# Attention read by state, then a squared-ReLU MLP, on one core: heads grouped by parity, w_in kept decoded on chip, scores and W2 of all batches in float32 on 64x32 tiles

## The chip, the cores and the metric

The kernel runs on one core of a Trainium2 chip. The core has a matrix engine (TensorE, PE in the profile, with its weight loads as PEld), a vector engine (VectorE, DVE), a scalar engine (ScalarE, ACT), a third elementwise engine (GpSimd, POOL) and SyncE (SP), which issues DMAs. Each engine takes its instructions strictly in the order in which they stand in its own queue; engines wait for one another with semaphores. Working memory is SBUF (128 partitions); matmul results go to PSUM, which this kernel uses as eight banks of 128 x 512 float32. The metric is the device time of the launch in microseconds.

## The reference

There are 8 batches of 8 heads, 512 tokens and 32 states per head, head width 64. `x` and `state` are float32, the two MLP weights are float64 (the launch passes them as pairs of 32-bit words).

```python
scores = scale * np.matmul(x, state.transpose(0, 1, 3, 2))      # [B,H,512,32]
a = softmax(scores);  xread = np.matmul(a, state)               # [B,H,512,64]
scores2 = scale * np.matmul(state, x.transpose(0, 1, 3, 2))     # [B,H,32,512]
a2 = softmax(scores2); sread = np.matmul(a2, x)                 # [B,H,32,64]
attn = np.concatenate([xread, sread], axis=2)                   # 544 rows per batch
x = attn.transpose(0, 2, 1, 3).reshape(B * 544, 512)
h = np.maximum(x @ w_in, 0.0)                                   # w_in [512,2048]
return (h * h @ w_out).astype(np.float32)                       # w_out [2048,512]
```

## The kernel before

**Algebra.** For the token rows, `xread @ w_in` is the sum over heads of `a_h @ (state_h @ w_in_h)`. The kernel therefore makes, for each batch, a small weight W2 = `state_h @ w_in_h` for all heads (256 rows: 8 heads x 32 states; 2048 columns) and multiplies the softmax `a` (256 rows by 512 tokens, tiles `k_hi`, `k_lo`) with it. The 256 rows of `sread` of all batches form a ninth block, number 8, which is multiplied with `w_in` itself.

**Number format.** A value is kept as two fast-format (float32r) parts: hi, a cast by ScalarE, and lo, the rest, subtracted by VectorE or GpSimd (`split`, L301). `mm3` (L317) makes a product of three matmuls: hi·hi, hi·lo, lo·hi. A plain float32 matmul is issued as two instructions.

**The MLP.** Block `b` has 16 steps `hidden.b.fc` (L733) of 128 hidden units each: 6 matmuls of 512 columns into a PSUM tile `ph`, ReLU (L744 or L748), squaring (ScalarE L745, or VectorE L749), the cast `g_hi` (L750, ScalarE) and the subtraction `g_lo` (L751, VectorE). `accumulate.b.fc` then does 12 matmuls of 512 columns into four PSUM tiles `acc`, which stay open over the 16 steps. In blocks 0 and 1 only steps 0 to 7 run at first; their partial sums go to DRAM (`keep_part`) and steps 8 to 15 follow later.

**Weights.** `decode` (L328) turns the float64 words into float32: one ScalarE instruction and four VectorE instructions (L333 to L336) on 128x512. There are 16 pieces of `w_in` (`decode_wi.p`) and 16 of `w_out` (`decode_wo`, `prep_wo.fc`). The decoded `w_in` is written to DRAM (`win_d`) and read back later.

**W2.** It is made in four ways. Batches 0 and 1, first half: `direct_w2` (L593), plain float32 with a block-diagonal state of 64 columns, so that the two head pairs use the two 64-column halves of the array. Batches 0 and 1, second half, and batches 6 and 7: `paired_w2` (L615) with `mm3`, two batches at once, stored in DRAM (`w2a_d`). Batches 2 to 5: `quad_w2` (L690), four batches at once, stored in DRAM (`w2_d`). `load_w2` reads a batch's weight back for its block; for batches 2 to 5 it is split again.

**Attention of a batch**, in two halves `g` of four heads: `prep` transposes x, `scores` multiplies it with a block-diagonal state (float32 for batches 0 and 1; `mm3` of six matmuls per half for the others), `transposed_scores` (L425), `softmax` (L450 to L468) and `exp_s` make both softmaxes, `transposes` and `sread` the second read.

**Order of the work.** `PLAN` is a table, written by hand, of all these steps; the framework's scheduler starts from it and interleaves the instructions of neighbouring steps. `SECOND` says for many steps which of two engines is to do a part. Buffers come from rotating pools; a step waits for the readers of its buffer's last content.

Of the kernel before, what the change touches and what calls it, by code (L numbers as in the profile page):

```python
# [18 lines left out]

# [3 lines left out]


PLAN = """
    zero_bd.0.1 zero_bd.0.0 zero_bd.1.0 load_wo.1 ident load_raw.0 load_direct start.0 load_raw.1 states
        prep.0.0 scores.0.0 transposed_scores.0.0 softmax.0.0 decode_wi.0 load.0.1 zero_bd.1.1
        prep.0.1 scores.0.1 exp_s.0.0 direct_w2.0 start.1 decode_wi.1 load_wo.2 load_wo.0
        load_raw.2 decode_wi.2 direct_w2.1 load_wo.4 transposes.0.0 sread.0.0 load_raw.3 prep_wo.0
        direct_w2.2 decode_wi.3 transposed_scores.0.1 softmax.0.1 load_wo.3 load.1.1 exp_s.0.1  # L30
        transposes.0.1
    hidden.0.0 prep_wo.1 sread.0.1 prep.1.0 direct_w2.3 prep_wo.2
    hidden.0.1 scores.1.0 load_wo.5 transposed_scores.1.0 load_raw.4 decode_wi.4 prep.1.1 accumulate.0.0
        load_raw.5 load_wo.6 prep_wo.3 decode_wi.5
    hidden.0.2 direct_w2.4 scores.1.1 transposed_scores.1.1 load_wo.7 accumulate.0.1 softmax.1.0
        load_raw.6 decode_wi.6 
    hidden.0.3 load_raw.7 prep_wo.4 decode_wi.7 direct_w2.5 prep_wo.6
    hidden.0.4 direct_w2.6 prep_wo.5 load_wo.8 direct_w2.7 accumulate.0.2 exp_s.1.0
    hidden.0.5 load_wo.9
    hidden.0.6 accumulate.0.3 softmax.1.1 prep_wo.7 load_raw.8 accumulate.0.4 decode_wi.8 prep_wo.8  # L40
        load_quad.0 prep_quad.0
    hidden.0.7 zero_bd.0.2 load_wo.11 qprep.0.8 load_raw.9 decode_wi.9 qprep.0.9 load_wo.10 accumulate.0.5
    hidden.1.0 exp_s.1.1 prep_wo.9
    hidden.1.1 load_wo.12 accumulate.0.6 transposes.1.0 qw2.0.8 accumulate.1.0 load_raw.10 decode_wi.10
        accumulate.0.7 load_raw.11 decode_wi.11
    hidden.1.2 sread.1.0 start.2 prep_wo.10 qprep.0.10 load_raw.12 decode_wi.12 accumulate.1.1 qprep.0.11
        qw2.0.9
# [180 lines left out]

# [738 lines left out]
```

## Time and profile before

| | |
|---|---|
| median of 2 runs | 727.3 us (726.02 to 728.57) |
| profiled execution, its own time | 726.54 us |
| its span in the profile | 724.8 us |
| busy: PE, DVE, ACT, POOL | 95%, 60%, 56%, 29% of the span |
| mean granted clock of PE | 0.988 |
| DMA | 105.26 MB in 90644 packets, mean 145 GB/s |
| HBM read, written | 68.42 MB, 36.18 MB |

The profile is of one execution. A page gives the busy time of each engine, then the span in 40 slices of 18.1 us, in which a digit is the busy share in tenths. Shares over the whole span hide that the kernel has stages: the first 170 us, in which the weights are decoded, look different from the rest, so the stages are read from a table of windows. A row of a group reads: line, engine, operation, output<-inputs, shape, count | busy us in total, mean ns of one | idle time ahead of it and what ended it. The time of one matmul in such a row is its whole passage through the array; in a dense row of matmuls the next one starts earlier than the last one ends.

### The profile page before, as it was taken

How to read it: one execution, taken by the hardware profiler on the slowest of the kernel's cores; microseconds unless marked ns; L12 is line 12 of the kernel's file. 1: busy time of each engine (PE TensorE's matmuls, PEld its weight loads, DVE VectorE, ACT ScalarE, POOL GpSimd, SP SyncE). 2: the span in 40 equal slices, each digit the busy share in tenths (PEclk: the TensorE clock that was granted, in tenths of full speed). 3: DMA queues.
4: the chain of work that ended last, by engine and by line, in shares of the span. 5: the costliest groups of instructions: out<-in, count | busy, mean ns of one | idle time of the engine just before them, and what ended most of it. 6: DMA issues, size and time to landing. Idle time of an engine off the chain costs nothing.

```text
span 724.8 us, 9841 instructions
## 1 busy us (share of the span) xinstructions
PE 685.3 (95%) x3288; PEld 561.8 (78%) x3288; DVE 432.3 (60%) x749; ACT 403.2 (56%) x787; POOL 213.5 (29%) x183
## 2 busy tenths in 40 slices
PE   5787888989999999999999999999999999999997
PEld 2454676768888788888888888888888888888886
DVE  3999999998735685355634574457448333332233
ACT  4766756676655467655556575555455463344333
POOL 1133724355161336404531251226003131011100
PEclk9999799999999999999999999999999999999999
DMA  9744379896873655352335233543355233424102
GB/s 277 207 169 137 116 246 298 272 244 191 232 249 102 215 163 162 104 189 73 99 106 167 81 117 100 173 124 113 102 165 183 59 87 91 114 60 102 30 0 88
DMA packets 90644, 105.26 MB, mean 145 GB/s; under 512 B 24801, under 2 KB 61665, under 8 KB 90593
## 3 DMA queue, kind: packets, MB, share of 16 engines
q1 hardware_dynamic: 90592, 104.63, 47.7%
q8 instruction: 26, 0.43, 0.2%
q14 instruction: 26, 0.20, 0.1%
HBM read 68.42 MB, written 36.18 MB: 144 GB/s over the span
## 4 chain that ended last, share of the span: by engine, by line
PE 73%; DVE 13%; DMA 6%; issue 3%; SPq 2%; ACT 2%; POOL 0%; DVEq 0%; ACTq 0%
PE acc L322 42%; PE ph L322 22%; PE pr L322 2%; PE st L322 2%; DMA xp<-in_x_dram 2%; DVE deco L335 2%; PE w2ps L322 2%; DMA decq<-win_d 1%; DVE dec L335 1%; DVE deco L336 1%; DVE dec L336 1%; DVE deco L333 1%; DVE dec L333 1%; DMA wi_raw<-in_moe_w_in_dram 1%; DMA w_d<-qo 1%
## 5 line engine op out<-in xcount | busy, mean ns | idle before, releaser
L322 PE MATMUL acc<-wo,g_hi 128*128 128x512 f32 x1088 | 320.6, 395 | 7.8 <-ACT g_hi L750 5.6
L322 PEld LDWEIGHTS acc<-wo,g_hi 128*128 128x128 f32 x1088 | 202.8, 190 | 51.8 <-ACT g_hi L750 7.6
L322 PE MATMUL acc<-wo,g_lo 128*128 128x512 f32 x544 | 191.0, 391 | 0.0
L322 PE MATMUL ph<-k_hi,w 128*128 128x512 f32 x512 | 181.6, 395 | 4.8 <-DVE g_lo L751 4.6
L751 DVE TENSOR_TENSOR g_lo<-ph,g_hi 128x512 fp32r<-128x512 f32 (+1 forms) x144 | 94.4, 656 | 87.9 <-ACT g_hi L750 85.5
L749 DVE SCALAR_TENSOR_TENSOR ph<-ph,r 128x512 f32<-128x512 f32 (+1 forms) x98 | 65.3, 667 | 93.3 <-ACT r L748 93.0
L322 PEld LDWEIGHTS ph<-k_hi,w 128*128 128x128 f32 x512 | 96.4, 189 | 29.9 <-DVE g_lo L751 7.9
L322 PEld LDWEIGHTS acc<-wo,g_lo 128*128 128x128 f32 x544 | 101.0, 188 | 19.8
L750 ACT CAST g_hi<-ph 128x512 fp32r<-128x512 f32 (+1 forms) x144 | 81.2, 564 | 49.8 <-DVE ph L749 48.6
L748 ACT ACTIVATE r<-ph 128x512 f32<-128x512 f32 (+1 forms) x98 | 56.5, 577 | 84.0 <-PE ph L322 83.7
L322 PE MATMUL ph<-k_lo,w 128*128 128x512 f32 x256 | 100.5, 393 | 0.6 <-DVE k_lo L304 0.6
L322 PEld LDWEIGHTS ph<-k_lo,w 128*128 128x128 f32 x256 | 48.3, 189 | 9.9 <-DVE k_lo L304 1.1
L744 ACT ACTIVATE ph<-ph 128x512 f32<-128x512 f32 (+1 forms) x46 | 25.5, 555 | 37.3 <-PE ph L322 37.2
L304 POOL TENSOR_TENSOR wi<-decq,wi 128x512 fp32r<-128x512 f32 x16 | 21.7, 1356 | 76.7 <-ACT wi L303 76.7
L304 POOL TENSOR_TENSOR w<-w_f,w 128x512 fp32r<-128x512 f32 x20 | 25.9, 1293 | 51.7 <-ACT w L303 51.6
L304 POOL TENSOR_TENSOR s<-decs,s 128x512 fp32r<-128x512 f32 x12 | 15.4, 1293 | 80.9 <-ACT s L303 80.8
L687 POOL TENSOR_TENSOR tt<-decq,tt 64x512 fp32r<-64x512 f32 x16 | 23.5, 1472 | 41.2 <-ACT tt L684 17.2
L304 POOL TENSOR_TENSOR xn_lo<-xn,xn_hi 128x1024 fp32r<-128x1024 f32 x10 | 24.0, 2401 | 25.5 <-ACT xn_hi L303 24.6
L304 POOL TENSOR_TENSOR x_lo<-xT,x_hi 128x512 fp32r<-128x512 f32 x11 | 14.3, 1301 | 48.1 <-ACT x_hi L303 38.2
L517 ACT ACTIVATE srd<-pr,r 32x64 f32<-32x64 f32 x64 | 19.6, 306 | 14.4 <-PE pr L322 11.9
L304 POOL TENSOR_TENSOR wo<-deco,wo 128x512 fp32r<-128x512 f32 x13 | 18.4, 1416 | 28.1 <-ACT wo L303 15.2
L303 ACT CAST w<-w_f 128x512 fp32r<-128x512 f32 x32 | 19.7, 615 | 12.4 <-DMA w_f<-w_d 7.8
(123 smaller groups left out, 982.0 us busy)
## 6 DMA issues: line engine op xcount, KB each, us to landing
w<-w2a_d SPq DMA_DIRECT2D x48, 256.0 KB, 4.1
wo_raw<-in_moe_w_out_dram SPq DMA_DIRECT2D x16, 512.0 KB, 5.1
wi_raw<-in_moe_w_in_dram SPq DMA_DIRECT2D x16, 512.0 KB, 4.3
decq<-win_d SPq DMA_DIRECT2D x32, 256.0 KB, 3.0
w_d<-qo SPq DMA_DIRECT2D x64, 128.0 KB, 2.6
out_dram<-o SPq DMA_DIRECT2D x32, 256.0 KB, 3.8
w_f<-w_d SPq DMA_DIRECT2D x32, 256.0 KB, 2.8
w2a_d<-w2h SPq DMA_DIRECT2D x24, 256.0 KB, 3.0
```

The lines of the kernel that those rows point to most:

```text
L303: nc.scalar.copy(hi, src)
L304: pick(key, nc.gpsimd, nc.vector).tensor_sub(lo, src, hi.bitcast(F32))
L322: m = nc.tensor.matmul(ps, l, r, start=first and i == 0, stop=last and i == len(seq) - 1)
L333: nc.vector.tensor_scalar(vf, vf, F64_HI_MIN, F64_HI_MAX, ALU.max, ALU.min)
L335: nc.vector.scalar_tensor_tensor(v, high, 0xC0000000, v, ALU.bitwise_and, ALU.bitwise_or)
L517: nc.scalar.mul(srd[q].rearrange("p e d -> p (e d)"), pr[q, h], r2[q])
L687: eng.tensor_sub(t[v, :, i], wf[u], t[u, :, i].bitcast(F32))
L744: nc.scalar.activation(ph, ph, AF.Relu)
L748: nc.scalar.activation(r, ph, AF.Relu)
L749: nc.vector.scalar_tensor_tensor(ph, ph, 0.0, r, ALU.max, ALU.mult)
L750: nc.scalar.copy(ghi, ph)
L751: nc.vector.tensor_sub(glo, ph, ghi.bitcast(F32))
```

## The change

**What it does.** Heads are grouped by parity instead of by number: half `g` holds heads `g, g+2, g+4, g+6`. With that, the transposed state of all batches, `stT`, has in partitions 0 to 63 the even heads and in 64 to 127 the odd ones, and a head's state (64 rows, 32 columns) is one 64x32 tile of the array: two row halves by four column quarters. `scores` and the new `make_w2` issue eight float32 matmuls, one a head, in `by_head`, which pins them one behind the other, odd and even heads alternating and going to different PSUM banks. All of `w_in` stays decoded in SBUF (`wi`, four tiles), so `win_d`, `w2_d`, `w2a_d` and their DMAs go, as do the block-diagonal states, `direct_w2`, `paired_w2`, `quad_w2` and `load_w2`. A call of `make_w2` makes W2 of one batch for four steps (512 columns; 256 for the first four calls of batch 0). x is loaded for batches 2 to 7 twice, as before, now in 16 DMAs of 64 KB (`load_p`, pieces of 128 bytes) and one of 1 MB. The x of batch 0 is loaded through ScalarE's queue. The results of `sread` are moved between partitions by 16 DMAs within the chip (`move_sread`). PSUM keeps four banks for `acc`, two for `ph`, and gives the last two to one tile `psb`, of which there is a single buffer now, used in turn by scores, W2, transposes and `sread`. Block 8 now runs ahead of block 7, not interleaved with it. `accumulate.b.fc` stands one hidden step behind, where it stood two behind in the middle blocks.

```diff
-    hidden.0.0 prep_wo.1 sread.0.1 prep.1.0 direct_w2.3 prep_wo.2
+    hidden.0.0 load_raw.4 load_raw.5 load_wo.2 load_wo.3 start.1 load_n.1.0 load_n.1.1 load_n.1.2 load_n.1.3
...
+STATES = ((0, 2), (2, 3), (5, 3))
+OB, KB, XB, E2B, RB, WB, GB = 4, 2, 2, 2, 2, 2, 3
...
-    ps_b = ctx.enter_context(tc.tile_pool(name="ps_b", bufs=2, space=bass.MemoryType.PSUM))
+    ps_b = ctx.enter_context(tc.tile_pool(name="ps_b", bufs=1, space=bass.MemoryType.PSUM))
...
-    win_d = tc.dram_tile([NHB, NC // 2, P, 2, HB], F32, name="win_d")
-    w2_d = [tc.dram_tile([4, 4, Ns, G, HB], F32, name=f"w2_d{hb}") for hb in range(NHB)]
+    stT = cp.tile([P, B, NC, Ns], F32, tag="stT", name="stT")
+    wi = [cp.tile([P, NC, 2 * HB], F32, tag=f"wi{n}", name=f"wi{n}") for n in range(NHB // 2)]
...
+    def banks(name):
+        return ps_b.tile([P, 2, S], F32, tag="psb", name=name)
...
+    def by_head(jobs):
+        for i, (ps, l, r) in enumerate(jobs):
+            with tc.high_priority() if i else nullcontext():
+                m = nc.tensor.matmul(ps, l, r, start=True, stop=True)
+            if i:
+                tc.keep_in_program_order(m)
...
+        def load_p(self, j):
+            b = self.b
+            if j == 0:
+                self.xp = p2.tile([P, NC, J, 32], F32, tag="x", name=f"xp{b}", bufs=XB)
+            for h in range(2):
+                for e in range(E):
+                    o = 64 * h + 32 * e
+                    nc.sync.dma_start(
+                        self.xp[o : o + 32, j],
+                        x[b, 2 * j + h].rearrange("(t s) d -> s t d", s=32)[:, :, 32 * e : 32 * e + 32],
+                    )
...
+        def scores(self):
+            b = self.b
+            t = banks(f"sc{b}")
+            for g in range(G):
+                self.st[g] = t[:, g]
+            jobs = []
+            for j in range(NC):
+                for g in (1, 0):
+                    d, q = slice(64 * g, 64 * g + 64), slice(32 * j, 32 * j + 32)
+                    jobs.append((self.st[g][q], stT[d, b, j], self.xT[d, j]))
+            by_head(jobs)
...
+    def make_w2(b, hb, n):
+        if hb % 2 == 0:
+            w2t[b] = p2.tile([P, 2, G, 2, HB], F32R, tag="w2", name=f"w2_{b}_{hb}", bufs=WB)
+        u = slice(hb % 2, hb % 2 + n)
+        w = w2t[b]
+        t = banks(f"w2ps{b}_{hb}")
+        ps = [t[:, g, : n * HB].rearrange("p (u f) -> p u f", u=n) for g in range(G)]
+        jobs = []
+        for j in range(NC):
+            for g in (1, 0):
+                d, q = slice(64 * g, 64 * g + 64), slice(32 * j, 32 * j + 32)
+                r = wi[hb // 2][d, j, HB * (hb % 2) : HB * (hb % 2 + n)]
+                jobs.append((ps[g][q].rearrange("p u f -> p (u f)"), stT[d, b, j], r))
+        by_head(jobs)
+        for g in range(G):
+            split_v(w[:, u, g, 0], w[:, u, g, 1], ps[g])
...
+    def move_sread():
+        t = p2.tile([P, NC, B * Ns], F32, tag="wraw", name="srn", bufs=RB)
+        for g in range(G):
+            for e in range(E):
+                for j in range(NC):
+                    o = 64 * g + 32 * e
+                    nc.sync.dma_start(t[o : o + 32, j], srall[32 * j : 32 * j + 32, 2 * g + e])
+        hi, lo = [p2.tile([P, NC, B * Ns], F32R, tag=t, name=f"sr_{t}", bufs=KB) for t in ("k_hi", "k_lo")]
+        split_v(hi, lo, t)
...
+            pick(f"load_n.{b}.{k}", nc.sync, nc.scalar).dma_start(
+                self.xn[:, k], x[b, :, ts(k, P)].rearrange("h p d -> p h d")
+            )
```

**How it moves instructions.** Three places show it.

VectorE, around the subtraction `g_lo_6` of step 6 of block 0. In the kernel before this stands there (`dec` is a piece of `w_in` in decoding, `deco` one of `w_out`, `g_lo` the end of a hidden step):

```order
L335 SCALAR_TENSOR_TENSOR dec_745<-wi_raw_731,dec_745 128x512
L335 SCALAR_TENSOR_TENSOR deco_752<-wo_raw_636,deco_752 128x512
L336 SCALAR_TENSOR_TENSOR dec_745<-wi_raw_731,dec_745 128x512
L751 TENSOR_TENSOR g_lo_6_692<-ph_6_684,g_hi_6_691 128x512
L336 SCALAR_TENSOR_TENSOR deco_752<-wo_raw_636,deco_752 128x512
```

In the changed kernel the place looks so (`w_0_2` is a part of batch 0's W2, `sc_609` the scores of batch 1, `sp_0` and `xT` their transposes and those of x of batch 2):

```order
L293 SCALAR_TENSOR_TENSOR deco_1205<-wo_raw_1082,deco_1205 128x512
L293 SCALAR_TENSOR_TENSOR deco_1249<-wo_raw_1129,deco_1249 128x512
L258 TENSOR_TENSOR w_0_2_408<-w2ps_3_567,w_0_2_408 128x256 x2
L373 STREAM_TRANSPOSE sp_0_618<-sc_609 128x512
L542 TENSOR_TENSOR g_lo_6_592<-ph_6_584,g_hi_6_591 128x512
L356 STREAM_TRANSPOSE xT_1375<-xp_1232 128x512 x4
L396 TENSOR_REDUCE m_0_620<-sp_0_618 128x16
```

`deco_1249` is the last of the 32 pieces: in the changed order all 32 decodings stand ahead of `g_lo_6` of block 0, and 15 of them ahead of `g_lo_0`. In the order before, 6 stand ahead of `g_lo_0` and 21 ahead of the first `g_lo` of block 1; the last ones stand behind the first `g_lo` of step 8.

PE, from the end of block 0's first half to the start of block 1. Before (`ph_0_824` and `ph_1_857` are the first hidden steps of block 1, `acc_0` belongs to block 0, `w2ps_8` and `pr_0` are W2 of the second half and the second read of batch 1):

```order
L322 MATMUL ph_0_824<-k_hi_223,w_1_0_218 128x512
L322 MATMUL acc_0_0_453<-wo_600,g_lo_6_692 128x512
L322 MATMUL acc_0_1_454<-wo_600,g_lo_6_692 128x512
L322 MATMUL acc_0_2_455<-wo_600,g_lo_6_692 128x512
L322 MATMUL acc_0_3_456<-wo_600,g_lo_6_692 128x512
L322 MATMUL w2ps_8_892<-wi_8_795,s_hi 128x256
L508 MATMUL pr_0_977<-xn_0_225,eTf_0_890 128x256 x2
```

After (`sc_609` again the scores of batch 1, `w2ps_0_712` the first W2 of batch 1, `ph_0_749` the first hidden step of block 1):

```order
L271 MATMUL ph_6_584<-k_hi_88,w_0_2_408 128x512
L279 MATMUL sc_609<-xT_496,stT 32x512 x8
L271 MATMUL ph_7_677<-k_hi_88,w_0_2_408 128x512
L271 MATMUL acc_0_0_285<-wo_674,g_hi_6_591 128x512 x2
...
L271 MATMUL acc_0_3_288<-wo_708,g_lo_7_685 128x512
L279 MATMUL w2ps_0_712<-wi_73,stT 32x512 x8
L271 MATMUL ph_0_749<-k_hi_250,w_1_0_711 128x512
```

The scores of batch 1, which stood far ahead of block 1, now stand 25 matmuls (one of `ph_7`, 24 of `acc`) and the first W2 ahead of it.

ScalarE, the head of its queue. Before (`dec` and `deco` are the first instructions of decodings, `bd` the block-diagonal state, `xTf` the copies of the transposed x of batch 0):

```order
L332 ACTIVATE dec_173<-wi_raw_116 128x512
L548 COPY bd_101<-stdT_132 64x2x32 x4
L548 COPY bd_102<-stdT_132 64x2x32 x4
L332 ACTIVATE dec_230<-wi_raw_130 128x512
L610 CAST w_0_0_217<-w2ps_212 128x256
L314 COPY xTf_0_142<-px_0_0_143 128x512
```

After:

```order
L330 DMA xn_90<-in_x_dram 128x8x64 x4
L288 ACT_TABLE_LOAD
L288 ACTIVATE dec_194<-wi_raw_81 128x512
L264 COPY xT_110<-px_0_111 128x512
L264 COPY xT_110<-px_1_117 128x512
L264 COPY xT_110<-px_2_123 128x512
L264 COPY xT_110<-px_3_129 128x512
L288 ACTIVATE dec_200<-wi_raw_99 128x512
```

The second decoding stands behind four copies of x of batch 0, each of which needs its whole `px` and so all four loads of x.

More of the change, by code (lines that the diff above doesn't have):

```diff
@@ L39 @@
[L39 to L47, printed above, removed]
@@ L403, in scores @@
[L403 to L419 removed]
+            self.k = [p2.tile([P, G, S], F32R, tag=t, name=f"{t}{b}", bufs=KB) for t in ("k_hi", "k_lo")]
@@ L704, in load_w2 @@
[L704 to L714 removed]
+        hb, i = divmod(p, 2)
@@ new lines, in decode_wi @@
+        to = wi[hb // 2][:, 2 * i : 2 * i + 2, ts(hb % 2, HB)]
+        decode(raw.pop(p), [2, HB], p, to.bitcast(U32))
+    w2t = {}
+    def make_w2(b, hb, n):
[14 more added lines that the diff above has]
+            split_v(w[:, u, g, 0], w[:, u, g, 1], ps[g])
+        for i in range(n):
+            weights[b, hb + i] = (w[:, hb % 2 + i, :, 0], w[:, hb % 2 + i, :, 1])
@@ L847, in tile_attn_moe @@
     step("ident", make_identity, nc, ident)
[L848 to L855 removed]
+    for b0, n in STATES:
+        step(key("load_states", b0), load_states, b0, n)
+        step(key("prep_states", b0), prep_states, b0, n, after=[key("load_states", b0)])
@@ L857, in tile_attn_moe @@
+    group = {b: b0 for b0, n in STATES for b in range(b0, b0 + n)}
     for b in range(B):
         early = b < NX
+        step(key("start", b), start, b)
+        for i in range(KC if early else 1):
+            step(key("load_n", b, i), lambda b, i: att[b].load_n(i), b, i, after=[key("start", b)])
+        loaded = [key("load_n", b, i) for i in range(KC if early else 1)]
+        for j in range(NC):
+            if not early:
+                step(key("load_p", b, j), lambda b, j: att[b].load_p(j), b, j, after=[key("start", b)])
+            need = loaded if early else [key("load_p", b, j)]
+            step(key("prep", b, j), lambda b, j: att[b].prep(j), b, j, after=need + [key("prep", b, j - 1)] * (j > 0))
@@ L859, in tile_attn_moe @@
         step(
-            key("start", b), start, b,
-            after=["ident"] if early else [key("zero_bd", b % 2, 1), key("zero_bd", b % 2, 2), key("scores", b - 2, 1)],
+            key("scores", b), lambda b: att[b].scores(), b,
+            after=[key("prep", b, j) for j in range(NC)] + [key("prep_states", group[b])],
         )
-        step(key("load", b, 1), lambda b: att[b].load(1), b, after=[key("start", b)])
         for g in range(G):
             after = {
-                "prep": [key("load", b, 1) if g else key("start", b)],
-                "scores": [key("prep", b, g), "states"],
-                "transposed_scores": [key("scores", b, g)],
+                "transposed_scores": [key("scores", b)],
```

816 lines of the change are left out of this document (273 added, 543 removed).

## The prediction

> **What bounds the kernel now.** I read the engine totals of the page first, then its slices, then a table of windows cut at the points where the slices change.
>
> ```profile
> PE 685.3 (95%) x3288; PEld 561.8 (78%) x3288; DVE 432.3 (60%) x749; ACT 403.2 (56%) x787; POOL 213.5 (29%) x183
> ...
> PE   5787888989999999999999999999999999999997
> DVE  3999999998735685355634574457448333332233
> ```
>
> Over the whole span PE is the bound. But eight slices of 18.1 us, from 18 to about 163 us, show DVE at nine tenths or more, and PE reaches that in one of them: there the order of the two is turned round. The windows say how far.
>
> ```profile
> core 0: us, PE busy (x) PEld busy (x) DVE busy (x) ACT busy (x) POOL busy (x), PEclk, DMA share, GB/s
> 0.00:18.00 18.00, 10.07 (x36) 4.34 (x37) 7.13 (x15) 7.16 (x17) 3.02 (x11) 1.00 0.98 277
> 18.00:45.00 27.00, 18.42 (x81) 11.38 (x79) 26.89 (x61) 20.88 (x49) 5.95 (x7) 0.90 0.72 225
> 45.00:99.50 54.50, 46.07 (x197) 33.51 (x195) 54.25 (x95) 32.61 (x66) 24.40 (x22) 0.89 0.38 128
> 99.50:145.10 45.60, 40.42 (x190) 32.58 (x191) 43.69 (x73) 30.55 (x60) 16.29 (x13) 1.00 0.92 290
> 168.80:724.80 556.00, 550.18 (x2697) 464.05 (x2696) 279.68 (x477) 295.15 (x570) 151.34 (x123) 1.00 0.41 122
> ```
>
> From 18 to 99.5 us DVE is idle for 0.4 us in 81.5: the decoding of the weights sets the time. From 168.8 us PE is busy for 550.18 of 556.00 us, and there only matmuls count. Two marks tie this to the program: `g_lo` of the first step of block 1, and that of the first step after block 0's second half has begun (step 12 of block 0).
>
> ```profile
> 99.46 0.68 DVE L751 TENSOR_TENSOR g_lo<-ph,g_hi 128x512 fp32r<-128x512 f32 x1
> 168.84 0.69 DVE L751 TENSOR_TENSOR g_lo<-ph,g_hi 128x512 fp32r<-128x512 f32 x1 [0.65 <-ACT g_hi L750]
> ```
>
> The profiled execution took 726.54 us, a span of 724.8 and 1.7 around it; the median of the two runs is 727.3. I add up the changed kernel's span by position in time, and put 1.7 on it.
>
> **The change, part by part. 1: the start.**
>
> ```profile
> 6.50 0.43 DVE L333 TENSOR_SCALAR dec<-dec 128x512 f32<-128x512 f32 x1 [5.10 <-ACT dec L332]
> 11.60 1.07 ACT L314 COPY xTf<-px 128x512 f32<-128x512 f32 x2
> 14.13 1.11 PE L391 MATMUL px<-ident,xn 128*128 128x128 f32 x4
> 16.54 0.66 PE L391 MATMUL px<-ident,xn 128*128 128x128 f32 x4
> xn<-in_x_dram SPq DMA_DIRECT2D x16, 128.0 KB, 2.7
> ```
>
> DVE gets its first decoding at 6.5 us and will here too. The second stands in ScalarE's new queue behind four copies of x of batch 0, and each copy needs all four loads of x (256 KB each, now on ScalarE's own queue, beside SP's loads of the raw weights). DVE therefore waits from about 9 us until x is in and copied. When x lands has no row: the lower bound is about 8 us (128 KB lands in 2.7 us; twice that behind an issue at 2 to 3 us). The upper one is 22 us, if x shares the queue time fairly with some 5.5 to 6 MB of loads at the first window's 277 GB/s. The nearest rows are the last transposes of batch 0's x, at 14.13 and 16.54 us; I take 15. Four transposes and four copies (half of 1.07 us each) add about 4: DVE goes on at 19.
>
> **2: the opening.** In the changed order all 32 decodings stand ahead of the scores of batch 1, some 165 DVE instructions behind the arrival of x; before, only 21 pieces stood ahead of the first `g_lo` of block 1, and the other eleven lay in the stage behind it. Pieces that lay behind that point are now ahead of it. The pace of DVE: 61 instructions in 26.89 us in the window from 18 us (0.44 each), 95 in 54.25 in the next (0.571). They differ because a decoding's operations stretch while POOL works, most where POOL is busy:
>
> ```profile
> L335 DVE SCALAR_TENSOR_TENSOR dec<-wi_raw,dec x16: 624/679/1644, 7.6 to 140.0; 128x512 uint32<-128x512 uint32 x16
> L304 POOL TENSOR_TENSOR wo<-deco,wo 128x512 fp32r<-128x512 f32 x13 | 18.4, 1416 | 28.1 <-ACT wo L303 15.2 <-DMA xn<-in_x_dram 11.4 <-issue 1.3
> ```
>
> One operation of the decoding takes 679 ns in the median and 1644 at most. POOL has 16 subtractions of `w_out` at 1.42 us in the new opening, some 25 us with the rest; from 18 to 145 us before it had 46.6. The two windows together give 156 in 81.14 = 0.52; I take 0.54, as W2's subtractions also come in: 165 x 0.54 = 89 us (73 to 94 by the two ends). With 3 us for waits between DMA, ScalarE and DVE, the scores of batch 1 are read by DVE at 19 + 89 + 3 = 111 us.
>
> **3: the softmax of batch 1, bare.**
>
> ```profile
> L425 DVE STREAM_TRANSPOSE sp<-st 128x512 f32<-128x512 f32 x16 | 11.4, 711 | 9.4 <-PE st L322 6.7 <-PE st L412 2.6
> L455 DVE TENSOR_REDUCE m<-sp 128x16 f32<-128x512 f32 x16 | 10.7, 669 | 0.0
> L456 POOL TENSOR_TENSOR sp<-sp,m 128x512 f32<-128x512 f32 x8 | 9.7, 1216 | 5.0 <-DVE nb L434 4.8
> L457 ACT ACTIVATE sp<-sp 128x512 f32<-128x512 f32 x16 | 10.2, 637 | 4.3 <-DVE sp L456 2.2 <-POOL sp L456 2.0
> L459 DVE TENSOR_REDUCE s<-sp 128x16 f32<-128x512 f32 x16 | 10.8, 676 | 2.7 <-ACT sp L457 2.7
> L462 POOL TENSOR_TENSOR sp<-sp,s 128x512 f32<-128x512 f32 x9 | 9.7, 1079 | 24.5 <-DVE s L461 20.7 <-ACT ph L744 3.8
> L465 DVE STREAM_TRANSPOSE aT<-sp 128x512 f32<-128x512 f32 x16 | 11.2, 700 | 2.9 <-POOL sp L462 2.7
> ```
>
> In the old order these steps of batch 1 stood far ahead of block 1, among block 0's matmuls. Now PE has 25 matmuls (5.7 us at the 0.227 us of part 5) and a W2 left between those scores and block 1. One half of the heads takes 0.71 + 0.67 + 1.22 + 0.64 + 0.68 + 1.08 + 0.70 and half a microsecond for two small operations = 6.2 us; `sp` has one buffer, so the halves follow each other: 12.4. Ahead of the maximum stand four transposes of x of batch 2 (4 x 0.7 = 2.8). Then come the first exponentials and the cast `k_hi` (1.8), four casts and subtractions of W2 (2.4), twelve matmuls (2.7), and ReLU, square and cast (2.5 to 3), with 0.5 for handing over: 25.5 us. The single buffer `psb` lies in the same chain, since W2 of batch 1 waits until the exponentials have read the scores. So the first `g_lo` of block 1 falls at 136.5 us where it fell at 99.46. Bounds: 18 if both halves overlap after all, 30 if each hand-over costs as much again.
>
> **4: to step 12 of block 0.** Before, 168.84 - 99.46 = 69.4 us, held back by DVE (43.69 of 45.60 us). With nothing left to decode PE sets it: 198 matmuls x 0.227 = 45, three groups of W2 and the second read (7): 52. This stage ends at 188.5, 20 us later than before. Part 2 and 3 thus cost 37 us and part 4 gives 17 back.
>
> **5: from there to the end.**
>
> ```profile
> 600.91 1.98 PE L322 MATMUL acc<-wo,g_hi 128*128 128x512 f32 x8
> 254.69 0.28 PE L697 MATMUL qps<-tt,s_hi 128*128 128x256 f32 x1
> 254.80 0.28 PE L698 MATMUL qps<-tt,s_lo 128*128 128x256 f32 x1
> L697 PE MATMUL qps<-tt,s_hi 128*128 128x256 f32 x58 | 15.1, 284 | 1.1 <-DVE qo L312 1.1
> L322 PE MATMUL w2ps<-wi,s_hi 128*128 128x256 f32 x64 | 13.0, 282 | 0.0
> L322 PE MATMUL st<-x_hi,bd_hi 128*128 128x512 f32 x20 | 7.8, 392 | 0.0
> 35.76 1.06 PE L412 MATMUL st<-xTf,bd 128*64 128x512 f32 x4
> 36.74 0.73 PE L322 MATMUL ph<-k_hi,w 128*128 128x512 f32 x2
> 17.12 1.08 PE L603 MATMUL w2ps<-dec,bd 128*64 128x256 f32 x8
> 21.26 1.99 PE L508 MATMUL pr<-xn,eTf 128*128 128x256 f32 x8 [0.68 <-ACT eTf L314]
> ```
>
> Eight dense matmuls of 512 columns take 1.98 us, less the last one's passage beyond its step: one every 0.227. Those of 256 columns start 0.11 to 0.12 apart. Removed: 116 of `qps` (the row and its like with `s_lo`) and 96 of `w2ps` (64 and 32) at 0.12, 60 of `st` (three rows of 20) at 0.227: 13.9 + 11.5 + 13.6 = 39.0 us. Added: 26 groups of W2 and 6 of scores, eight heads each. What a group costs has no row. Nearest is `st`: two float32 matmuls (four instructions) on two column halves, and the next matmul starts 0.98 later. That column tiles run side by side shows in the last two rows, 1.08 against 1.99 us for the same eight instructions. If all eight tiles do, a group is 0.98; if the two row halves follow each other, 2.0. No row shows row halves; I take 1.2, near the `st` row with something for a second set of weights: 32 x 1.2 = 38.4 (31 to 64). So 556.0 - 39.0 + 38.4 = 555. The Trainium skill, "TensorEngine Tiling (Array Packing)", Key Properties, says that different tiles load weights and multiply in parallel, which gives the 0.98 and 7 us less; it also says that a change of tiling mode drains the array, which speaks against 32 groups among 128x128 matmuls. The `st` row has one such change inside its 0.98.
>
> Costed at nothing: the DMAs within the chip and the two loads of x (DMA is at 0.41 in this stage, and the round trips of W2 and `w_in` go); and the accumulation one step behind, whose 18 matmuls of cover (4.1 us) lie over a chain of four operations of about 0.6 us each. If that cover goes, a step loses a part of a microsecond.
>
> Sum: 188.5 + 555 + 3 for the clock and block 8's ends = 746.5; with 1.7, **748 us**.
>
> **The rivals.** *A: the opening keeps DVE's fast pace* and the kernel is not slower. POOL has half the work there, so DVE could hold 0.44 an instruction: 165 x 0.10 = 16 us less, 732. It decides once the mean of the opening's DVE instructions falls below 0.50. The window from 18 us speaks for it (POOL at 5.95 of 27 us), the stretch in the next against. *B: x of batch 0 comes late*, by its upper bound of 22 us: 7 us more, 755, with a small loss behind it up to 759. For it speaks the DMA share of 0.98 in the first window; against it that x lay in the same crowd before and was there by 14. The Trainium skill, "DMA: Bandwidth & Descriptors", section "Queues, rings and completion order", has each DMA engine go round-robin between the queues it has work for, by packets; by that ScalarE's queue would get its half and x come early. *C: the row halves do not run side by side*, so the change does not do what it says: 35 groups x 0.8 = 28 us more, 776. For it: no row shows them. Against: the column tiles. *D: faster by over 2%*: nothing priced here gets below 713; it needs A, the low ends of parts 1 and 3, and 0.98 at once.
>
> **How the numbers follow.** The forecast has 0.49 with a range of its own of 738 to 762, A 0.26, B 0.11, C 0.10, D 0.04. About 2% (712.8 to 741.8) is what a measurement of this kernel tells from no change. Same: A and the 0.06 of the forecast below 741.8, 0.32. Slower: 0.64. The range reaches from 731, in the middle of A, to 781, the upper side of C; it leaves out D, the lower part of A and the extreme of C, some 0.18.
>
> **What would show it.** Right: DVE near full until about 111 us; the copies of x at about 15 us and DVE idle before them; first `g_lo` of block 1 near 136; PE idle for 10 to 15 us around the scores of batch 1; groups of 1.2 us; 555 us from step 12 of block 0 to the end. Wrong: a first `g_lo` of block 1 before 120 (A), copies of x behind 20 us (B), groups near 2 us (C), or PE waiting for `g_lo` in the middle blocks, where the accumulation's cover was priced at nothing.

## The result, and the profile after

The changed kernel takes 748.9 us (median of two runs, 748.75 and 748.96) against 727.3: 1.030 times as long, with a 95% interval of 1.022 to 1.037. The forecast was 748.0 with a range of 731 to 781. Its profiled execution took 748.75 us, a span of 746.9.

The totals of the page and its slices, now of 18.7 us (the last row is the clock that PE was granted; the trace has no entry of it before 53.2 us, so its first three digits say nothing):

```profile
PE 676.3 (91%) x3536; PEld 519.1 (69%) x3536; DVE 399.1 (53%) x712; ACT 328.5 (44%) x612; POOL 122.5 (16%) x86
...
PE   4047964999999899999999999999999999999997
...
DVE  4999966223474563556355635564556445224332
...
PEclk9997977999999999999999999999999999999999
```

PE is busy for 9 us less than before (676.3 against 685.3), and the span is 22 us longer: what came is idle time of PE, nearly all of it in the first seven slices. DVE is full in four slices only, where it was full in eight. The windows, cut at the points of which the prediction spoke:

```profile
0.00:13.30 13.30, 6.45 (x30) 3.60 (x32) 2.70 (x6) 4.62 (x8) 0.70 (x6) 1.00 0.98 250
13.30:103.60 90.30, 47.07 (x222) 30.88 (x212) 89.44 (x163) 48.61 (x90) 24.17 (x16) 0.91 0.59 186
103.60:135.40 31.80, 18.90 (x96) 11.49 (x96) 14.99 (x33) 13.43 (x28) 9.23 (x8) 0.77 0.28 73
135.40:189.60 54.20, 54.17 (x275) 42.21 (x276) 16.36 (x27) 25.73 (x50) 0.00 (x0) 1.00 0.25 59
189.60:746.90 557.30, 549.73 (x2923) 430.89 (x2921) 275.62 (x486) 236.08 (x440) 88.40 (x56) 1.00 0.15 37
```

The marks on VectorE, `g_lo` of the first step of block 1 and of step 12 of block 0:

```profile
135.41 0.69 DVE L542 TENSOR_TENSOR g_lo<-ph,g_hi 128x512 fp32r<-128x512 f32 x1 [4.86 <-ACT g_hi L541]
189.57 0.69 DVE L542 TENSOR_TENSOR g_lo<-ph,g_hi 128x512 fp32r<-128x512 f32 x1 [0.65 <-ACT g_hi L541]
```

| | before | after | difference |
|---|---|---|---|
| to the first `g_lo` of block 1 | 99.5 us | 135.4 | +35.9 |
| from there to step 12 of block 0 | 69.4 | 54.2 | -15.2 |
| from there to the end | 556.0 | 557.3 | +1.3 |
| span | 724.8 | 746.9 | +22.1 |

How the opening ends is seen in PE's own rows from 94 us on (the number in brackets is the idle time ahead of the row and what ended it):

```profile
94.54 0.66 PE L353 MATMUL px<-ident,xn 128*128 128x128 f32 x4 [0.74 <-ACT srd L446]
95.88 0.66 PE L353 MATMUL px<-ident,xn 128*128 128x128 f32 x4 [0.68 <-ACT xT L264]
98.29 1.12 PE L353 MATMUL px<-ident,xn 128*128 128x128 f32 x4 [1.76 <-ACT xT L264]
100.08 1.11 PE L353 MATMUL px<-ident,xn 128*128 128x128 f32 x4 [0.68 <-ACT xT L264]
101.87 1.11 PE L279 MATMUL w2ps<-wi,stT 64*32 64x256 f32 x16 [0.68 <-ACT xT L264]
104.64 0.80 PE L271 MATMUL ph<-k_hi,w 128*128 128x512 f32 x1 [1.66 <-ACT w L257]
...
108.83 1.09 PE L279 MATMUL sc<-xT,stT 64*32 64x512 f32 x16
...
125.06 1.96 PE L279 MATMUL w2ps<-wi,stT 64*32 64x512 f32 x16 [8.53 <-ACT e L384]
```

From the second read of batch 0 (`srd`) to the first W2 of batch 1, each of these rows but that of the scores waits for the copy that empties `psb` after the one ahead of it. The wait of 8.53 us is for `e`, the exponentials that read the scores last. This row of steps was only half in the prediction: the part behind the scores stood there, the part ahead of them did not.

### The profile page after: what moved, and what is told of

The parts are those of the page before. It is cut to its first block, busy times and chain, and to the rows that moved or that the text cites. A ratio compares the mean times of both kernels' runs of the same rounds, so it can differ in the third digit from the quotient of the medians.

```text
span 746.9 us, 9406 instructions
## 1 busy us (share of the span) xinstructions
PE 676.3 (91%) x3536; PEld 519.1 (69%) x3536; DVE 399.1 (53%) x712; ACT 328.5 (44%) x612; POOL 122.5 (16%) x86
## 4 chain that ended last, share of the span: by engine, by line
PE 80%; DVE 12%; ACT 2%; issue 2%; DMA 2%; POOL 1%; ACTq 1%; DVEq 0%; POOLq 0%; SPq 0%
PE acc L271 47%; PE ph L271 25%; PE w2ps L279 4%; PE pr L271 2%; DVE dec L291 2%; DVE deco L291 1%; DVE wi L293 1%; DVE deco L293 1%; DMA wi_raw<-in_moe_w_in_dram 1%; DVE dec L289 1%; PE pt L423 1%; DVE deco L289 1%; DMA xn<-in_x_dram 1%; PE sc L279 1%; DVE deco L290 1%
## 5 line engine op out<-in xcount | busy, mean ns | idle before, releaser
L271 PE MATMUL acc<-wo,g_hi 128*128 128x512 f32 x1088 | 306.0, 398 | 12.1 <-ACT g_hi L541 12.1
L271 PE MATMUL acc<-wo,g_lo 128*128 128x512 f32 x544 | 175.6, 394 | 0.4 <-DVE g_lo L542 0.4
L540 DVE SCALAR_TENSOR_TENSOR ph<-ph,r 128x512 f32<-128x512 f32 (+1 forms) x125 | 82.8, 663 | 167.2 <-ACT r L539 166.9
L539 ACT ACTIVATE r<-ph 128x512 f32<-128x512 f32 (+1 forms) x125 | 71.3, 571 | 187.3 <-PE ph L271 187.3
L254 POOL TENSOR_TENSOR xs<-xn,xs 128x1024 fp32r<-128x1024 f32 x12 | 28.8, 2398 | 319.5 <-ACT xs L253 319.5
L279 PE MATMUL w2ps<-wi,stT 64*32 64x512 f32 (+1 forms) x544 | 37.9, 617 | 36.7 <-ACT e L384 34.4
L258 DVE TENSOR_TENSOR w<-w2ps,w 128x512 fp32r<-128x512 f32 (+1 forms) x68 | 44.4, 652 | 17.8 <-ACT w L257 17.5
L257 ACT CAST w<-w2ps 128x512 fp32r<-128x512 f32 (+1 forms) x68 | 38.3, 563 | 21.6 <-DVE w L258 16.7
L254 POOL TENSOR_TENSOR s<-wi,s 128x1024 fp32r<-128x1024 f32 x8 | 19.2, 2398 | 62.6 <-ACT s L253 62.6
L254 POOL TENSOR_TENSOR k_lo<-aT,k_hi 128x512 fp32r<-128x512 f32 x16 | 21.0, 1314 | 28.8 <-ACT k_hi L253 28.8
L271 PE MATMUL ph<-sr_k_hi,s 128*128 128x256 f32 x128 | 25.6, 283 | 0.0
L446 ACT ACTIVATE srd<-pr,r 32x64 f32<-32x64 f32 x64 | 19.5, 305 | 13.8 <-PE pr L271 11.4
```

What stands on the lines that cost most here:

```text
L254: pick(key, nc.gpsimd, nc.vector).tensor_sub(lo, src, hi.bitcast(F32))
L257: nc.scalar.copy(hi, src)
L258: nc.vector.tensor_sub(lo, src, hi.bitcast(F32))
L271: m = nc.tensor.matmul(ps, l, r, start=first and i == 0, stop=last and i == len(seq) - 1)
L279: m = nc.tensor.matmul(ps, l, r, start=True, stop=True)
L446: nc.scalar.mul(srd[q].rearrange("p e d -> p (e d)"), pr[q, j], r2[q])
```

## The experiments

Theory W is the prediction's: VectorE's decoding, all 32 pieces ahead of block 1, sets the opening, and a bare softmax of 25 us is added to it. Rival T puts the loss into the tiled groups and the shared buffer.

**1. Hold the 16 later pieces back.** The first instruction of each is pinned behind the steps that precede it in `PLAN`:

```diff
-        nc.scalar.activation(vf, high.bitcast(F32), AF.Abs)
+        m = nc.scalar.activation(vf, high.bitcast(F32), AF.Abs)
+        if late:
+            tc.keep_in_program_order(m)
```

> The changed kernel with one thing added: the 16 later pieces (w_in 8 to 15, w_out 8 to 15) may not be decoded ahead of the steps they stand behind in the plan. Theory W (the opening is VectorE's work, and all 32 pieces lie ahead of block 1): about 100 DVE instructions instead of 165 are left between the arrival of x and the scores of batch 1; at 0.56 us each they end at about 70 us, and then block 0's own matmuls are late: scores of batch 1 at 80 to 88 us (110 before), first g_lo of block 1 at 105 to 113 us (135.4). The 64 decoding instructions return as 36 us of DVE work in the stage to step 12 of block 0, which grows from 54 to 58 to 66 us. Time 726 to 736. Rival T (PE's own sharing of one PSUM buffer by scores, W2 and second read, and the tiled float32 groups, make the opening long): first g_lo of block 1 moves by less than 5 us, time 743 or more.

Measured: 754.4 us, 1.035 times the kernel before (1.029 to 1.041). VectorE does become free: `g_lo` of step 5 comes at 79.9 us instead of 90.5. But the scores are read at 100 us, not at 80 to 88, and block 1 starts at 124.9. PE's rows in that stretch, and a window of it, in which VectorE (third) is busy for 21.29 of 65.00 us:

```profile
85.60 0.66 PE L355 MATMUL px<-ident,xn 128*128 128x128 f32 x4 [0.43 <-ACT srd L448]
86.93 0.66 PE L355 MATMUL px<-ident,xn 128*128 128x128 f32 x4 [0.68 <-ACT xT L264]
...
90.92 1.11 PE L279 MATMUL w2ps<-wi,stT 64*32 64x256 f32 x16 [0.68 <-ACT xT L264]
...
97.54 1.17 PE L279 MATMUL sc<-xT,stT 64*32 64x512 f32 x16
...
114.10 1.96 PE L279 MATMUL w2ps<-wi,stT 64*32 64x512 f32 x16 [8.51 <-ACT e L386]
...
187.13 1.93 PE L279 MATMUL w2ps<-wi,stT 64*32 64x512 f32 x8 [5.06 <-DVE wi L295]
...
60.00:125.00 65.00, 49.49 (x257) 34.47 (x241) 21.29 (x45) 26.34 (x54) 8.02 (x7) 0.84 0.21 49
```

From step 5 to block 1 it is 45.0 us here, with VectorE mostly idle, and 44.9 us in the changed kernel, with VectorE full for the first 13 of them. That the two agree to 0.1 us is in part chance (run 4 has 50.0). Counted from the first transposes of x of batch 1 it is 39.3 us here and 40.9 in the changed kernel: that stretch is a serial chain and hardly a matter of VectorE's load. The last row of PE shows the price of the edit: a W2 waits for a piece of `w_in` decoded late, and the stage from block 1 to step 12 takes 72.8 us. Block 1 moves by 10.5 us, where theory W wanted 22 to 30 and rival T less than 5. Theory W holds up to step 5, which comes 10.6 us earlier, and falls behind it.

**2. Batch 1's softmax earlier; 3. both.** The second read of batch 0 moves ahead of step 2, and x, scores and softmax of batch 1 ahead of step 3:

```diff
+    transposes.0.0 sread.0.0 transposes.0.1 sread.0.1
     hidden.0.2 accumulate.0.1 prep_wo.2 load_raw.6 load_raw.7 load_wo.4 load_wo.5
+    prep.1.0 prep.1.1 prep.1.2 prep.1.3 scores.1 transposed_scores.1.0 softmax.1.0 transposed_scores.1.1 softmax.1.1
+    exp_s.1.0 exp_s.1.1
     hidden.0.3 decode_wi.4 prep_wo.3 accumulate.0.2 decode_wi.5 w2.0.2
```

> The changed kernel with the second read of batch 0 and then x, scores and both softmaxes of batch 1 planned three to four hidden steps earlier; all decodings stay ahead. Theory W (DVE's work ahead of block 1 plus a bare chain of 25 us): DVE has the same work and some 20 instructions of the softmax more before block 1, and the chain lies inside it: DVE full until about 115 us, first g_lo of block 1 at 116 to 123 us instead of 135.4, time 729 to 737. Rival T: with one PSUM buffer the scores of batch 1 only hold up the W2 of batch 0 earlier, and block 1 starts at 130 or later, time 743 or more.

> Both edits together. Theory W: DVE's work ahead of block 1 is about 125 instructions (70 us at 0.56) behind the 13 us of the start, so the first g_lo of block 1 falls at 90 to 104 us; the stage to step 12 is 58 to 66 us long; time 714 to 728, that is at or below the kernel before the change. Rival T: above 735.

Measured: 759.3 us (1.042, 1.038 to 1.046) and 757.2 us (1.040, 1.036 to 1.044); block 1 starts at 143.6 and 127.1. Both miss what theory W expected, in direction too. What rival T had said of the buffer came instead: the scores now take `psb` while the W2 for step 4 still needs it, and that W2 waits behind them, 20.2 us in the first and 13.4 us in the second:

```profile
115.57 1.11 PE L280 MATMUL w2ps<-wi,stT 64*32 64x256 f32 x16 [20.21 <-ACT e L385]
```

```profile
98.78 1.11 PE L280 MATMUL w2ps<-wi,stT 64*32 64x256 f32 x16 [13.38 <-ACT e L387]
```

The first fence is the run without the hold, the second the run with it. From here on theory C stands beside W: behind step 5 it is the chain through the one buffer that sets the opening, and moving the scores only moves where it stands.

**4. The low parts of `w_out` on VectorE**, which measures the pace of the decoding by itself:

```diff
 SECOND = """
+    w_out_lo: 0 1 2 3 4 5 6 7 8 9 10 11 12 13 14 15
```

> The changed kernel with the 16 subtractions of the low part of w_out on VectorE instead of GpSimd. Theory P (each GpSimd operation stretches one operation of the decoding by about 1.07 us, which is what lifts the pace from 0.44 to 0.56 us): 16 x 1.07 = 17 us of stretch go, 16 x 0.60 to 0.68 = 10 us of subtractions come: DVE ends its opening about 7 us earlier, no decoding operation above 0.8 us but at GpSimd's few other operations, first g_lo of block 1 at 127 to 130 us, time 740 to 744. Rival N (the number of VectorE's instructions sets the pace, and the long ones have another cause): 10 us later, first g_lo of block 1 at 145, time 757 to 760.

Measured: 742.0 us (1.019, 1.015 to 1.023), block 1 at 128.4: 7.0 us earlier, as theory P expected. One operation of the decoding, in the changed kernel and in this one (count: shortest, median and longest in ns):

```profile
L291 DVE SCALAR_TENSOR_TENSOR deco<-wo_raw,deco x16: 644/678/1756, 16.9 to 101.7; 128x512 uint32<-128x512 uint32 x16
```

```profile
L292 DVE SCALAR_TENSOR_TENSOR deco<-wo_raw,deco x16: 650/681/685, 16.8 to 98.8; 128x512 uint32<-128x512 uint32 x16
```

All 128 decoding instructions together take 70.0 us instead of 84.9. In the changed kernel 16 of them are stretched, each beside an operation of GpSimd: 14 of the 16 subtractions of `w_out` (the last two come when the decoding is over) and two of `k_lo`. In this run none is; the two `k_lo` are still there, but fall beside other instructions of VectorE. That makes 14.9 us for 16, 0.93 each. The price is no fixed one: each of the 16 ends 0.28 us (the instructions that take 0.42 alone) or 0.55 us (those that take 0.68) behind the end of GpSimd's operation, as if it had waited for that. One pair of the changed kernel, GpSimd until 97.03 us, VectorE until 97.59:

```profile
95.21 1.82 POOL L254 TENSOR_TENSOR wo<-deco,wo 128x512 fp32r<-128x512 f32 x1 [3.46 <-ACT wo L253]
95.83 1.76 DVE L291 SCALAR_TENSOR_TENSOR deco<-wo_raw,deco 128x512 uint32<-128x512 uint32 x1
```

The subtractions cost VectorE 12.0 us, so the decoding itself ends only some 3 us earlier. The first transposes of x of batch 1 come 6 us earlier (88.5 us instead of 94.5), presumably because the steps ahead of them are served sooner on VectorE; no run shows that by itself. From there to block 1 it is 40.0 us, the chain of run 1 again. Step 5 comes 12.1 us earlier, but the second read behind it then waits 2.81 us for a copy on VectorE. The size was foreseen, the way to it only in part. The Trainium skill, "GPSIMD Engine Reference", section "Key points", says that GpSimd shares its SBUF interfaces with VectorE and contends with instructions of VectorE in a two-port mode or with two SBUF inputs; the 16 rows agree, and they put the price that this page does not give at about 0.9 us for one GpSimd operation of 1.3 to 2.2 us. Not every instruction of such a form beside GpSimd is held up: one of L291 takes its usual 0.68 us from 89.93 us on, while GpSimd is shown at work from 89.58 to 91.74.

**5. Block 1 reads batch 0's softmax.** This takes away what block 1 waits for, and does the same work later.

```diff
-            ks[blk] = att[blk].k
+            ks[blk] = att[0 if blk == 1 else blk].k
...
+    scores.1 transposed_scores.1.0 softmax.1.0 transposed_scores.1.1 softmax.1.1 exp_s.1.0 exp_s.1.1
     hidden.1.3 accumulate.1.2 decode_wi.10 prep_wo.9 load_raw.12 load_wo.11 decode_wi.11 w2.0.4
```

> The changed kernel, but block 1 multiplies with the softmax of batch 0 instead of its own (its rows of the result are batch 0's scores with batch 1's W2), and the scores and softmaxes of batch 1 are made four hidden steps later, under block 1's matmuls. All work is still done; only the wait of block 1 for its own softmax is gone. Theory C (with the decoding out of the way, what holds block 1 back is a serial chain, x of batch 1, W2, step 6, scores, softmax, W2, each waiting for the last through the one buffer psb; 45 us from g_lo of step 5 to block 1, the same 45.0 in the run that holds the late pieces back): the part from the scores on, 25 us, shrinks to a W2 and a hidden step, so the first g_lo of block 1 falls at 117 to 124 us and the time at 731 to 739. Theory W (DVE's decoding alone holds block 1): all 32 pieces are decoded by 104 us as before and block 1 starts no earlier than 130, time 743 or more.

Measured: 740.3 us (1.013, 1.009 to 1.017); block 1 at 124.0, just at the edge of what theory C expected, and well before the 130 of W. The time lies 1 us above C's range (731 to 739) and below W's 743. The gain is 11.4 us at block 1 and 8.6 in the end: the next stage takes 59.6 us instead of 54.2, since work has moved into it. PE has 302 matmuls there, where it had 275, and waits for 1.2 us:

```profile
124.00:183.60 59.60, 58.42 (x302) 44.21 (x303) 26.25 (x50) 28.24 (x58) 6.74 (x6) 1.00 0.32 75
```

**6. Two buffers of one bank** in place of one of two banks:

```diff
-    ps_b = ctx.enter_context(tc.tile_pool(name="ps_b", bufs=1, space=bass.MemoryType.PSUM))
+    ps_b = ctx.enter_context(tc.tile_pool(name="ps_b", bufs=2, space=bass.MemoryType.PSUM))
-        return ps_b.tile([P, 2, S], F32, tag="psb", name=name)
+        return ps_b.tile([P, S], F32, tag="psb", name=name)
```

> The changed kernel with psb as two buffers of one PSUM bank each (one per half of the heads) instead of one buffer of two: one part of the change undone. Theory C: transposes of x of batch 1, second read and W2 can be prepared in one bank while the other is read; four hand-overs of x and two of the second read between steps 5 and 6 fall under one another, 4 to 10 us of the 45; scores and W2 still need both. First g_lo of block 1 at 125 to 131 us, time 739 to 745. Theory W: no change beyond 3 us (746 to 751).

Measured: 763.2 us (1.046, 1.041 to 1.050), the slowest of all. In the opening theory C holds: block 1 starts at 129.3, 6 us earlier. But the first half of a middle block, steps 0 to 7, now takes 39.5 us where it took 36.9, and a whole one 79.1 where it took 75.5. The reason is in the groups of scores and W2, which the scheduler could now cut, since a group's first head waits for one bank only:

```profile
403.54 1.04 PE L278 MATMUL sc<-xT,stT 64*32 64x512 f32 x2
404.51 2.11 PE L270 MATMUL acc<-wo,g_hi 128*128 128x512 f32 x8
...
406.55 1.08 PE L278 MATMUL sc<-xT,stT 64*32 64x512 f32 x14
407.56 0.73 PE L270 MATMUL acc<-wo,g_lo 128*128 128x512 f32 x2
```

One head (two instructions) keeps the array for 0.97 us, and the other seven together for 1.01. That answers the prediction's rival C without a run of its own: the eight tiles, row halves included, run side by side, and a group costs one of them. In a middle block three of five groups are cut, which makes 2.9 of the 3.6 us. Two banks with uncut groups were not run, so what the second buffer is worth by itself stays open.

**7. Block 0 in one piece**, its chain under steps 8 to 15, and no partial sums in DRAM; **8.** the same with edits 4 and 6.

```diff
-    hidden.1.0
-    hidden.1.1 accumulate.1.0 load_wo.8 load_wo.9 decode_wi.8 w2.1.2 decode_wi.9
+    hidden.0.8 accumulate.0.7 prep_wo.8 prep.1.0 prep.1.1 prep.1.2 prep.1.3 scores.1 load_wo.12
+    hidden.0.9 accumulate.0.8 prep_wo.9 transposed_scores.1.0 softmax.1.0 decode_wi.12 load_wo.13 load_raw.14
...
+    hidden.0.11 accumulate.0.10 decode_wi.14 decode_wi.15 w2.0.6 prep_wo.11 load_wo.15 load_states.2
```

> The changed kernel with the first blocks planned otherwise: block 0 runs its 16 steps in one piece, then block 1, so no partial sums go to DRAM; x, scores and softmax of batch 1 lie under steps 8 to 15 of block 0. The decodings and every matmul stay. Theory C: VectorE still decodes until about 104 us and step 7 of block 0 ends near there, but PE then has block 0's second half to do while the chain of batch 1 runs: the 18 us of idle PE between 93 and 135 us go, and part of the matmuls at half clock: time 722 to 732, near the kernel before the change. Theory W: DVE's work is the same and PE waits as long for it; time 740 or more.

> Block 0 in one piece, the low parts of w_out on VectorE, and psb as two single banks, together. Theory C: the gains add up, for the pace of the decoding (7 us as measured), the chain (18 or more) and the hand-overs are different stretches of the same opening: 711 to 724, below both kernels. If they are one and the same stretch, the second and third give nothing: 725 to 732.

Measured: 750.0 us in both (1.027, 1.023 to 1.031), 18 us above the range of theory C in the first, and 18 to 26 above its two ranges in the second. The scores stood ahead of the W2 for step 12, and the same wait is there again, under another name:

```profile
131.80 1.09 PE L277 MATMUL sc<-xT,stT 64*32 64x512 f32 x16
...
146.28 1.96 PE L277 MATMUL w2ps<-wi,stT 64*32 64x512 f32 x16 [10.43 <-ACT e L382]
```

In the first, step 11 comes at 130.7 us and step 12 at 157.1; the second has the wait too, and the cut groups of run 6 on top. So the plan was wrong by the theory's own terms, and the next two runs, whose edit is shown against run 7, put it right.

**9. The W2 for step 12 ahead of the scores**, and the transposes of x of batch 1 behind steps 6 and 7; **10.** the same with edit 4.

```diff
+    prep.1.0 prep.1.1
-    hidden.0.6 accumulate.0.5 prep_wo.6 load_wo.8 load_wo.9 decode_wi.8 decode_wi.9 load_raw.10 load_raw.11
+    hidden.0.6 accumulate.0.5 prep.1.2 prep.1.3 prep_wo.6 load_wo.8 load_wo.9 decode_wi.8 decode_wi.9 load_raw.10 load_raw.11
...
-    hidden.0.8 accumulate.0.7 prep_wo.8 prep.1.0 prep.1.1 prep.1.2 prep.1.3 scores.1 load_wo.12
+    hidden.0.8 accumulate.0.7 prep_wo.8 load_wo.12 decode_wi.12 load_raw.14 decode_wi.13 load_raw.15 decode_wi.14 decode_wi.15 w2.0.6
+    hidden.0.9 accumulate.0.8 prep_wo.9 scores.1 load_wo.13
```

> Block 0 in one piece as before, but the W2 of its steps 12 to 15 is now made ahead of the scores of batch 1 (the buffer psb was held by them for 26 us while step 12 waited), and the transposes of x of batch 1 stand behind steps 6 and 7 instead of behind nothing. Theory C: the chain of batch 1's softmax lies under steps 11 to 15 (some 22 us of matmuls over 18 to 20 us of chain); no gap over 5 us in PE between step 7 of block 0 and step 15; first g_lo of block 1 at 146 to 156 us (175.6 in the run before), time 722 to 732. If the 26 us had another cause than the held buffer, the gap is there again and the time 745 or more.

> The same with the low parts of w_out on VectorE. Theory C: DVE's decoding still sets the pace up to step 6 of block 0, so the 7 us of the single edit come off again: first g_lo of block 1 at 138 to 149 us, time 712 to 725. If with the chain covered the pace of the decoding no longer decides, no gain over the run beside it.

Measured: 736.9 us (1.010, 1.007 to 1.013) and 730.7 us (1.001, 0.999 to 1.003). The gap of 26 us is gone in both; in the first, step 11 comes at 134.7 and step 12 at 138.4. Both times lie 5 to 6 us above the range expected, because block 1 starts at 166.5 and 160.7, later than foreseen. Here are the windows of the second, around that place:

```profile
103.00:145.20 42.20, 41.01 (x208) 30.61 (x208) 25.81 (x50) 19.20 (x35) 6.78 (x6) 0.95 0.11 26
145.20:160.70 15.50, 12.32 (x80) 8.43 (x78) 3.86 (x7) 7.74 (x19) 0.00 (x0) 1.00 0.23 76
```

PE is dense from step 7 to step 15, with batch 1's chain under it, and then the first W2 of batch 1 and its second read hand `psb` over one after the other. With the changed kernel's arithmetic untouched, the order alone takes 12 us off (748.9 to 736.9), and the engine choice of edit 4 six more; then no difference from the kernel before can be measured.

**11. x of batch 0 on SP's queue**, a single run:

```diff
 SECOND = """
-    load_n: 0.0 0.1 0.2 0.3
```

> The changed kernel with the four loads of x of batch 0 on SP's queue among the raw loads, as before the change, instead of ScalarE's. The second decoding waits for the copies of x, on whichever queue it came. By the prediction's term x arrives at 8 to 22 us; on ScalarE's queue it was in at about 10. Theory: on SP's queue it lands at 10 to 14 us, the second decoding starts 0 to 4 us later, and the first g_lo of block 1 moves by the same 0 to 4 us (135 to 140), since VectorE is full from there. If the start does not matter, because the opening waits on the chain, block 1 moves by less than 1 us although the second decoding moves.

Measured: 748.05 us in its one run; the second decoding starts at 13.6 us instead of 13.3, block 1 at 134.6. The queue on which x comes decides nothing that this one run can show.

**12. The step from block 0 to block 1.** The first W2 of batch 1 goes ahead of its second read, the softmax of batch 1 onto VectorE alone, and the squares of block 1 to VectorE; the edit is against run 10:

```diff
-    hidden.0.12 accumulate.0.11 prep_wo.12 transposes.1.0 sread.1.0 start.2 load_p.2.0 load_p.2.1 load_p.2.2 load_p.2.3
+    hidden.0.12 accumulate.0.11 prep_wo.12 w2.1.0 start.2 load_p.2.0 load_p.2.1 load_p.2.2 load_p.2.3
...
+    hidden.1.1 accumulate.1.0 w2.1.2 transposes.1.0 sread.1.0 prep.2.1 load_n.2.0
```

> As the run with block 0 in one piece, its chain covered and the low parts of w_out on VectorE; and in addition the first W2 of batch 1 stands ahead of batch 1's second read (four transposes, second read and its four scalings held psb between g_lo of step 15 and block 1, 15 us with 4 us of idle PE and matmuls at half clock behind it), the softmax of batch 1 runs on VectorE alone, and block 1's squares go back to VectorE. Theory C: g_lo of step 15 to the first g_lo of block 1 shrinks from 15.5 us to 8 to 11, and with it the time by 4 to 8 us: 722 to 728, below the kernel before by up to 1%. What the second read now does between steps 3 and 8 of block 1 has 3 us to spare before the W2 of steps 8 and 12; if it holds them up, that takes the gain back (729 to 735).

Measured: 733.9 us (1.008, 1.005 to 1.011). Step 15 to block 1 takes 9.0 us, as expected, and block 1 starts at 151.8, 8.9 us earlier than in run 10. But step 8 of block 1 comes at 194.5 (198.0 there) and block 2 at 239.0 (235.2): block 1 takes 87.2 us instead of 74.5. PE has more to do in it (82.2 us busy against 74.5, with the second read moved in) and waits for 5.0 us where it had not waited, longest for 2.73 us on `g_hi` of step 8, behind the scores of batch 2. So the time falls into the second branch of the expectation (729 to 735); that `psb` is what PE waits for there is not shown, and three edits at once do not tell which one costs it. No version that was run beats the kernel before.

## Why the prediction was right, and where only its sum was

**The sum was right to 1 us** (748.0 against 748.9), and by stages: block 1 at 136.5 forecast and 135.4 measured; 52 and 54.2 us to step 12; 558 (555 and 3 for the clock and the ends) and 557.3 us to the end. What it said of the cause holds at the top: PE has less to do, and the loss lies ahead of block 1, where PE waits. Inside the first stage two of its terms were off and cancelled, which is luck: the scores of batch 1 were to be read at 19 + 89 + 3 = 111 us, and they were at 13.3 + 90.3 + 6.4 = 110.0, the 6.4 us being mostly waits behind PE's chain, which the sum does not have.

**The start was sized too long.** It took x of batch 0 to arrive at 15 us and DVE to go on at 19. The copies ran at 10.6 us and DVE went on at 13.3:

```profile
10.64 2.05 ACT L264 COPY xT<-px 128x512 f32<-128x512 f32 x4 [2.77 <-PE px L353]
13.29 0.43 DVE L289 TENSOR_SCALAR dec<-dec 128x512 f32<-128x512 f32 x1 [2.55 <-ACT dec L288]
```

DVE did wait for the copies, as said, but went on 6 us sooner; rival B, a late x, fell with it.

**The pace was right.** From 13.3 to 103.6 us VectorE runs 163 instructions in 90.3 us, 0.554 each, where 0.54 was taken; rival A needed less than 0.50. That GpSimd stretches the decoding is shown by run 4, not only argued. Run 4 is no test of A's 732, though its mean is 0.498 (182 instructions in 90.6 us): it takes 14.9 us of stretch away and puts 12.0 us of subtractions in its place. That a faster VectorE would not have won all that A counts on is seen from run 1.

**The step that failed is that VectorE alone holds the scores of batch 1 until 111 us.** VectorE was through with the decoding at 103.6 us, and after two short subtractions for W2 it waited 4.1 us for PE:

```profile
102.33 1.28 DVE L293 SCALAR_TENSOR_TENSOR deco<-wo_raw,deco 128x512 uint32<-128x512 uint32 x2
...
110.02 0.72 DVE L373 STREAM_TRANSPOSE sp<-sc 128x512 f32<-128x512 f32 x1 [4.12 <-PE sc L279]
```

What it waited for is the part ahead of the scores: second read, four transposes of x through one buffer, W2, step 6. It follows the matmuls of step 5. From the first of these transposes to block 1 it is 40.9 us, and 39.3 with VectorE mostly idle (run 1). The prediction had `psb` in the chain behind the scores alone. So its numbers would have misled as advice: taking 64 decoding instructions out of the opening, worth 36 us by the pace, brought block 1 forward by 10.5 us and made the kernel slower in the end (754.4 us).

**The bare softmax was right**: scores read at 110.0 us, first `g_lo` of block 1 at 135.4, 25.4 us where 25.5 was summed. Run 5 shows it as a cause: without the wait block 1 starts 11.4 us earlier. It is less than 25, since W2 and a hidden step remain and the rest of PE's chain is there as before.

**The groups were priced right.** Forecast 1.2 us, from rows without row halves; measured in block 1, and the same in the middle blocks:

```profile
143.50 0.39 PE L271 MATMUL ph<-k_hi,w 128*128 128x512 f32 x1
143.82 1.09 PE L279 MATMUL w2ps<-wi,stT 64*32 64x512 f32 x16
144.84 1.20 PE L271 MATMUL acc<-wo,g_hi 128*128 128x512 f32 x4
145.88 0.39 PE L271 MATMUL acc<-wo,g_lo 128*128 128x512 f32 x1
```

A group occupies 1.02 us. The matmul ahead of it runs 0.32 to the group's start instead of 0.227, 0.09 more, and the four behind it take 1.04 instead of 0.91, some 0.13 more: about 1.24 in all. The Trainium skill, "TensorEngine Tiling (Array Packing)", Key Properties, was weighed for both: that tiles work in parallel agrees with the 1.02, and that a change of tiling mode drains the array with the 0.09 and 0.13, less than a fifth of the group's price. Rival C is out. So the sum of this stage holds by its parts: 39.0 us removed and 38.4 added left PE 0.6 us less to do, and it is busy for 549.73 us where it was for 550.18. The stage is 1.3 us longer all the same, since PE is idle for 7.6 us of it where it was for 5.8; 3 had been put for that. It also means that the change takes nothing off PE where PE is the bound: 8.5 of the 9 us that PE is less busy lie ahead of step 12 of block 0, where it waits anyway.

**Costed at nothing, and it was**: the accumulation one step behind. In the last stage PE is busy for 549.73 of 557.30 us, and it waits for `g_lo` for 0.4. The copies within the chip and the loads of x left no wait either.

## What to carry to other kernels

When a change saves matmuls and gives one PSUM buffer to four kinds of work, write down the order in which that buffer changes hands, step by step with its readers, and look for stretches where nothing else is queued on the matrix engine: here the order was worth 12 us (748.9 to 736.9). An engine that is full for 90 us can hide such a chain; take its load away and measure, and the chain is what remains. More than half of the loss was the order, and a better order gave that back: block 0 in one piece and the W2 ahead of the scores that hold its buffer brought 1.030 down to 1.010, and 16 subtractions moved to another engine to 1.001. And read a saving by stage before you count on it: of 9 us less for PE, half a microsecond lay where PE sets the time.
